# A gated scan and a two-layer product on one core: v released by the first piece of alpha, a new written order for all engines at the start, and idle products ahead of four steps

## The chip, the cores and the metric

The kernel runs on one core of a Trainium2 chip. The metric is the device time of one execution in microseconds; before the change it is 177.0, the median of 5 runs (176.86 to 177.19). A core has five engines with queues of their own: TensorE (PE in the profile, its weight loads PEld), VectorE (DVE), ScalarE (ACT), GpSimd (POOL) and SyncE (SP). Each works through its own instructions in program order and waits for the others through semaphores. SP, ACT and POOL also issue DMA transfers.

## The reference, cut to what matters

A scan over 768 steps for 4 batches and 8 heads of width 48, then two products with a GELU between them:

```python
for t in range(S):
    state = alpha[:, :, t, :, None] * state + np.einsum('bhd,bhe->bhde', k[:, :, t], v[:, :, t])
    y[:, :, t] = np.einsum('bhd,bhde->bhe', q[:, :, t], state)
x = np.ascontiguousarray(y.transpose(0, 2, 1, 3)).reshape(B * S, H * D)      # 3072 x 384
h = x @ w_in                                                                  # 384 -> 2048
g = 0.5 * h * (1.0 + np.tanh(c * (h + 0.044715 * h * h * h)))
return (g @ w_out).astype(np.float32)                                         # 2048 -> 384
```

Inputs and output are float32.

## The kernel before, in words

**Tiling.** The 768 steps are cut into 6 chunks of 128. A "pair" is one chunk of two batches, so there are 12 pairs, numbered in the order of the chunks: pairs 0 and 1 are chunk 0. In a chunk the scan is done with matrix products. ScalarE takes the logarithm of alpha (`ln`, L359/L361), TensorE sums it along the steps with a triangular matrix (`cum`, L346 to L380), ScalarE takes the exponentials b, binv and bend of the sums (L401, L407), VectorE scales q by b and k by binv (`qp`, `kp`, L418). TensorE turns both (`t`, L428), a copy brings them to SBUF (`ev`, L446), TensorE forms the products of all step pairs (`attn`, L489), VectorE masks them to the lower triangle (`mask`, L496). TensorE makes y from the masked products and v, and from chunk 1 on also from the carried state (`y`, L543, L546); kv (L506) and st (L528, L531) carry the state on. y is cast (`x`, L553), turned (`tx`, L560) and copied (`xe`, L564) to xT. In pairs 0 and 1, which are loaded in a packed form, k is also turned back (L454, L461), and v comes in float32 and is cast by a copy (`vb`, L389).

**The two layers.** `l1` is layer 1 (L572, tile hT): groups of six products of 256 columns, each followed by a GELU on ScalarE (L578). Eight groups make a pair. w_in comes in four pieces; group n of a pair needs piece n // 2, and all x of its pair. `l2` is layer 2 (L591, tile acc): four products of 384 columns a group; w_out comes in four pieces as well. `ot` copies a result out (L603) and SP stores it. Chunk 0's two pairs share their layer 2.

**PSUM.** Three kinds of banks: `ca` (one double bank, sums and products), `yk` (two: turns, y, kv, x turns) and `ff` (four: hT, acc, and the sums and products of the first pairs). A task that takes a bank waits for the one that used it before.

**Loads.** The alpha, q and k of pairs 0 and 1 come in twelve loads of 192 KB, ten from SP's queue and two (the first q and k) from ScalarE's: the "ring". They are named `load.0` to `load.11`. Everything else goes through POOL's queue in the order of `LOADS`: v of pair 0 (`load.12`), the first piece of w_in, v of pair 1, the other three pieces, w_out and the rows of later pairs. Two `gate` tasks stand in this queue. A gate is a copy of one column (L314) on POOL out of a tile that a ring load fills: it waits for that load, so all that POOL issues behind it waits too. `gatea 0 1` reads the second half of pair 0's alpha, and stands ahead of v; `gatek 0 1` reads the second half of pair 0's k, and stands ahead of w_in. From the ninth transfer on POOL waits for the landing of the one eight earlier before it issues.

**Order.** All work is added as tasks to a `Scheduler`, which fixes every engine's program. The list `FIRST` is taken first, word for word: `P:` is TensorE, `V:` VectorE, `A:` ScalarE, `G:` POOL, `S:` SP, and `fill.n` are n idle products of 512 columns of zeros in an ff bank (L289). Behind the list the scheduler goes on by itself, task by task, by priority and by planned times; for these it uses `COST`, `LAT`, and for the loads the planned landings in `LANDED`. A task that can run on ScalarE or VectorE goes where the list puts it.

Of the kernel before, what the change touches and what calls it, by code (L numbers as in the profile page):

```python
# [171 lines left out]
class _Kernel:  # L172
# [3 lines left out]

    SPLIT = (2,)
    EARLY = (0, 1)
    LOADS = ('gatea 0 1', 'v0', 'gatek 0 1', 'in 0', 'v1', 'in 1', 'in 2', 'in 3', 'out 0', 'out 1', '2a', 'out 2', '2b', 'out 3', '3', '4', '5', '6', '7', '8', '9', '10', '11')

    PACKED, CUM_FF, R = (0, 1), (0, 1), 4
    RINGS = (('a', 0, 0, 1), ('a', 0, 1, 2), ('q', 0, 0, 1), ('k', 0, 0, 1), ('q', 0, 1, 2), ('k', 0, 1, 2),
             ('a', 1, 0, 1), ('a', 1, 1, 2), ('q', 1, 0, 1), ('k', 1, 0, 1), ('q', 1, 1, 2), ('k', 1, 1, 2))
    BY_ACT = (2, 3,)

    FIRST = """
        A:table.0 A:load.2 A:load.3 S:load.0 S:load.1 S:load.4 A:ln0.0 S:load.5 P:fill.7 P:cum0.0 A:ln0.1 G:gate.0 G:load.12 S:load.6 P:cum0.1 A:b0.0 S:load.7
        A:bend0.0 V:qp0.0 A:binv0.0 A:binv0.1 S:load.8 V:kp0.0 P:fill.2 P:t0.0 A:b0.1 V:ev0.0 P:fill.1 P:t0.1 S:load.9 A:ev0.1 V:qp0.1 S:load.10 A:bend0.1
        P:fill.3 P:attn0.0 V:kp0.1 G:gate.1 S:load.11 P:t0.2 G:load.13 V:mask0.0 A:ev0.2 P:t0.3 G:load.14 V:mask0.1 A:ev0.3 P:fill.1 P:t0.4 V:ev0.4 P:fill.1
        P:attn0.1 A:ln1.0 G:load.15 P:t0.5 V:mask0.3 P:cum1.0 A:ev0.5 G:load.16 V:vb0.0 A:ln1.1 V:end0.0 P:y0.0 V:mask0.2 G:load.17 P:kv0.0 A:binv1.0 P:cum1.1  # L190
        V:st0.0 A:x0.0 G:load.18 A:vb0.1 V:kp1.0 P:tx0.0 A:b1.0 P:y0.1 V:xe0.0 G:load.19 V:qp1.0 P:t1.1 A:x0.1 A:bend1.0 G:load.20 A:b1.1 P:fill.1 P:t1.0
        A:ev1.0 V:ev1.1 G:load.21 V:qp1.1 P:fill.1 P:kv0.1 V:st0.1 G:load.22 A:binv1.1 P:tx0.1 P:attn1.0 V:xe0.1 G:load.23 P:t1.2 V:kp1.1 P:l10.0 A:ev1.2
        G:load.24 V:mask1.0 P:t1.3 A:bend1.1 P:t1.4 V:mask1.1 G:load.25 A:ev1.3 P:l10.1 V:ev1.4 G:load.26 A:vb1.0 P:t1.5 P:attn1.1 G:load.27 V:ev1.5 P:y1.0
        G:load.28 P:l10.3 V:end1.0 V:vb1.1 V:mask1.2 G:load.29 A:gelu0.0 P:kv1.0 P:l10.2 V:mask1.3 A:x1.0 G:load.30 P:l10.5 A:gelu0.1 V:st1.0 A:gelu0.3 P:y1.1
        G:load.31 P:l10.4 A:gelu0.5 V:x1.1 P:tx1.0 A:gelu0.2 P:tx1.1 P:l10.6 G:load.32 V:xe1.1 A:gelu0.4 V:xe1.0 P:l10.7 A:gelu0.6 G:load.33 P:l11.0 A:gelu0.7
        P:l11.6 A:gelu1.0 P:l11.5 A:gelu1.6 P:l11.7 A:gelu1.5 P:l11.2 A:gelu1.7 P:l11.4 A:gelu1.2 P:l11.3 A:gelu1.4 P:l11.1 A:gelu1.3 P:kv1.1 P:l20.0
        A:gelu1.1 P:l20.4 P:l20.1 A:ln2.0 P:l20.2 P:cum2.0 P:l20.5 A:b2.0 A:binv2.0 P:l20.9 A:bend2.0 V:kp2.0 A:ln2.1 P:l20.6 V:st1.1 P:cum2.1 V:qp2.0 P:l20.8
        A:b2.1 A:binv2.1 P:t2.0 P:l20.3 V:kp2.1 A:ev2.0 V:qp2.1 P:l20.10 A:bend2.1 P:attn2.0 P:t2.1 V:mask2.1 P:l20.7 A:ev2.1 V:mask2.0 P:l20.14 A:ln3.0
        P:attn2.1 P:y2.0 V:mask2.2 P:l20.13 V:mask2.3 P:l20.12 V:x2.0 P:cum3.0 A:ot0.0 V:ot0.1 P:y2.1 A:ot0.2 S:store0.0 S:store0.1 P:tx2.0 P:l20.11 A:x2.1
        S:store0.2 V:xe2.0 A:b3.0 P:tx2.1 P:l20.15 V:xe2.1 A:binv3.0 V:end2.0 P:l12.0 V:ot0.3 A:bend3.0 P:l12.1 V:qp3.0 S:store0.3 P:kv2.0 P:l12.2 V:st2.0  # L200
        A:gelu2.0 P:l12.3 V:end3.0 V:kp3.0 A:gelu2.1 P:l12.4 A:gelu2.2 P:t3.0 A:gelu2.3 P:t3.1 A:gelu2.4 V:ev3.0 P:l12.5
    """.split()
    LANDED = {"load.0": 2800, "load.1": 3400, "load.2": 4400, "load.3": 5000, "load.4": 6000, "load.5": 7300, "load.12": 10100, "load.6": 9200, "load.7":
              10000, "load.8": 10500, "load.9": 11000, "load.10": 11600, "load.11": 12000, "load.13": 14100, "load.14": 16000, "load.15":
              17800, "load.16": 19200, "load.17": 21100, "load.18": 23500, "load.19": 24800, "load.20": 26400, "load.21": 27100, "load.22":
              27900, "load.23": 28300, "load.24": 30100, "load.25": 31000, "load.26": 31900, "load.27": 32600, "load.28": 32900, "load.29":
              34800, "load.30": 36700, "load.31": 38400, "load.32": 41200, "load.33": 42600}

    NARROW = (0, 1)

# [12 lines left out]
                a=6, q=5, k=5, vb=6)  # L223
# [60 lines left out]
    def fill(self, n):  # L284
# [4 lines left out]
                self.nc.tensor.matmul(ps, self.zero[:, 0:self.C], self.zero, start=True, stop=True)  # L289
        return emit  # L290


    def load(self, n, c, i, lo=0, hi=2):

# [202 lines left out]
                                         self.ut[:, None, :].to_broadcast([self.C, self.H // 2, self.C]), op=ALU.mult)  # L497
        return emit

    def kv(self, u, i):  # L500
        nc, H, C, D = self.nc, self.H, self.C, self.D

        def emit(e):
            kv = u["kv", i] = self.tile("yk", [C, H // 2, 2 * D], F32, "kv")
            for p in range(H // 2):
                nc.tensor.matmul(kv[:, p, :], u["kn" if u["packed"] else "kp"][:, i, 2 * p:2 * p + 2, :].rearrange("t h d -> t (h d)"),  # L506
                                 u["vb"][:, i, 2 * p:2 * p + 2, :].rearrange("t h d -> t (h d)"),
                                 start=True, stop=True)
        return emit
# [25 lines left out]
    def y(self, u, i, c, b):  # L535
        nc, H, C, D = self.nc, self.H, self.C, self.D

        def emit(e):
            y = u["y", i] = self.tile("yk", [C, H, D], F32, "yps")
            if c > 0:  # L540
                st = self.state[b][c % 2]
                for p in range(H // 2):
                    nc.tensor.matmul(y[:, 2 * p:2 * p + 2, :], u["T"][:, 0, i, p, :], st[:, p, :],  # L543
                                     start=p == 0, stop=False, skip_group_check=True)
            for h in range(H):
                nc.tensor.matmul(y[:, h, :], u["atm", i][:, h % 2, h // 2, :], u["vb"][:, i, h, :],  # L546
                                 start=c == 0, stop=True, skip_group_check=True)
        return emit
# [4 lines left out]
            self.copy(e)(x, u["y", i].rearrange("t h d -> t (h d)"))  # L553
        return emit

    def turn_x(self, u, i):
        def emit(e):
            ps = u["xT_ps", i] = self.tile("yk", [self.C, self.NKT, self.C], BF16, "xT_ps")
            for j in range(self.NKT):
                self.nc.tensor.transpose(ps[:, j, :], u["x", i][:, j * self.C:(j + 1) * self.C], self.ident)  # L560
        return emit
# [57 lines left out]
    def tasks(self):  # L619
        s = self.s = Scheduler(self.BUFS, self.fill, 60000, self.FIRST, self.LANDED)  # L620
# [6 lines left out]
        loads, n, gate, held = {}, 0, [], {}  # L627
# [43 lines left out]
        for m, (c, i) in enumerate(pairs):  # L671
# [81 lines left out]
            for j in range(2):  # L753
                b, o, k, ms, turned = 2 * i + j, P + 10 + 3 * j, kp[j], masks[j], turns[j]
                at = ats[m][-1 if m not in self.SINGLE else j]
                y = s.add("y", {"PE": W["intra"] + (W["inter"] if c else 0)}, P + 20 + j, self.y(u, j, c, b),
                          ms + turned + [vin[j]] + ([states[b, c - 1]] if c else []))
                xc = s.add("x", {"ACT": W["xc_act"], "DVE": W["xc"]}, P + 20 + j, self.x(u, j), [y])
                if m in self.TURN_X:
                    xe = tx = s.add("turn", {"SP": W["turn"]}, P + 22 + j, self.turn_x_dma(u, j, c, b), [xc], xbar=W["xbar_x"], late=W["late_x"] * (m < 6))  # L760
                else:
                    tx = s.add("tx", {"PE": W["tx"]}, P + 22 + j, self.turn_x(u, j), [xc])
                    xe = s.add("xe", {"DVE": W["xe"]}, P + 22 + j, self.turned_x(u, j, c, b), [tx])
                    tx.take("yk", xe)
                y.take("yk", xc)
                xc.take("x", tx)
                users += [at, y]
                ms[0].take("atm", y)
                xts[c, b], ys[b, c] = xe, y
                vs.append(y)  # L770
                if c < NCH - 1:
                    if u["packed"]:
                        tb = s.add("t", {"PE": W["t4"]}, P + 29 + j, self.turn_back(u, j), turned)
                        k = s.add("ev", {"DVE": W["ev4"], "ACT": W["ev4_act"]}, P + 29 + j, self.turned_back(u, j), [tb])
                        tb.take("yk", k)
                        users.append(tb)
                        backs.append(tb)
                    kv = s.add("kv", {"PE": W["kv"]}, P + 30 + j, self.kv(u, j), [k, vin[j]])
                    st = states[b, c] = s.add("st", {"DVE": W["st" if c else "st0"]}, P + 30 + j, self.carry(u, j, c, b),
                                              [kv, end] + ([states[b, c - 1], ys[b, c - 1]] if c else []))  # L780
                    kv.take("yk", st)
                    vs.append(kv)
                    kvs.append(kv)
                    cs.append(st)
# [136 lines left out]
```

## Time and profile before

| | |
|---|---|
| time, median of 5 runs | 177.0 us (176.86 to 177.19) |
| the profiled execution | 177.78 us |
| its span on the core | 176.0 us |
| TensorE busy | 170.9 us (97%) |
| ScalarE, VectorE, POOL busy | 128.8, 96.4, 57.6 us |
| TensorE's share of the chain that ended last | 86% |
| DMA's share of it | 9% |
| granted TensorE clock | 1.00 |

The span runs from the first to the last instruction; 1.78 us of the profiled time lie around it. Most of TensorE's time is layer 1 (69.7 us in 576 products) and layer 2 (69.0 us in 416). "Busy" of TensorE is modelled from pipelined products, so a product counts longer than the distance to the next one, and small gaps don't show in it; the chain of work that ended last gives the distances. In a row of the timeline the first number is the start, the second the length, and what stands in brackets is the idle time of the engine just before, with what ended it. For a DMA that ScalarE, SP or POOL issues, the row is the issue; the transfer lands later.

### The profile page before, as it was taken

What the parts mean: (1) busy time and instruction counts of PE and PEld (TensorE: products, weight loads), DVE (VectorE), ACT (ScalarE), POOL (GpSimd) and SP (SyncE); (2) the same over time, 40 slices, a digit from 0 to 9 for tenths busy, and PEclk for the clock granted to TensorE, in tenths of its full rate; (3) what the DMA queues carried; (4) which work ended last, traced back from release to release, by engine and by line L of the source; (5) the groups of instructions that cost most, each with busy time, mean ns of one, the idle gap of its engine ahead of it and who ended that gap; (6) DMA issues with size and microseconds to landing.
All of it is one profiled execution on the core that took longest, in us unless ns stands there. A gap on an engine that the chain in (4) does not pass through costs nothing.

```text
span 176.0 us, 4440 instructions
## 1 busy us (share of the span) xinstructions
PE 170.9 (97%) x1845; PEld 135.1 (77%) x1845; DVE 96.4 (55%) x192; ACT 128.8 (73%) x213; POOL 57.6 (33%) x64
## 2 busy tenths in 40 slices
PE   7999899999999999999999999999999999999993
PEld 2576799666886897797698698688697697796973
DVE  6599720265878994696598797494436405000000
ACT  4677979766968668858788967977988984481841
POOL 2495447987645766667530000000000000000000
PEclk9999999999999999999999999999999999999999
DMA  4999999999999999999999993371271360301102
GB/s 141 312 246 219 210 242 238 236 211 206 230 291 206 236 262 217 216 224 204 196 257 231 200 114 98 63 171 49 47 180 34 89 164 4 108 27 48 45 0 89
DMA packets 49620, 28.86 MB, mean 164 GB/s; under 512 B 37696, under 2 KB 46016, under 8 KB 49600
## 3 DMA queue, kind: packets, MB, share of 16 engines
q0 software_dynamic: 26464, 17.70, 60.8%
q1 hardware_dynamic: 22592, 10.49, 24.8%
q10 hardware_dynamic: 544, 0.39, 0.8%
q8 instruction: 14, 0.23, 0.6%
q14 instruction: 6, 0.05, 0.1%
HBM read 25.17 MB, written 4.72 MB: 170 GB/s over the span
## 4 chain that ended last, share of the span: by engine, by line
PE 86%; DMA 9%; POOL 2%; SPq 1%; issue 0%; ACT 0%; POOLq 0%
PE acc L591 36%; PE hT L572 35%; DMA w_in<-in_moe_w_in_dram 6%; PE at L489 3%; DMA k<-in_k_dram 3%; PE qkT_ps L428 3%; PE yps L546 2%; PE yps L543 2%; PE cum L378 2%; PE kv L506 2%; SPq L305 1%; PE xT_ps L560 1%; POOL w_in L321 1%; PE cum L380 1%; POOL v L308 1%
## 5 line engine op out<-in xcount | busy, mean ns | idle before, releaser
L572 PE MATMUL hT<-xT,w_in 128*128 128x256 bf16 x576 | 69.7, 273 | 0.5 <-DMA w_in<-in_moe_w_in_dram 0.5
L578 ACT ACTIVATE gT<-hT 128x512 bf16<-128x512 f32 x96 | 56.4, 598 | 18.5 <-PE hT L572 15.1
L591 PE MATMUL acc<-w_out,gT 128*128 128x384 bf16 (+3 forms) x416 | 69.0, 313 | 0.0
L572 PEld LDWEIGHTS <-w_in 128*128 128x128 bf16 x576 | 61.0, 114 | 2.5 <-DMA w_in<-in_moe_w_in_dram 0.8
L591 PEld LDWEIGHTS <-gT 128*128 128x128 bf16 x416 | 36.9, 97 | 19.2
L496 DVE TENSOR_TENSOR atm<-at,ut 128x512 bf16<-128x512 f32 x48 | 30.1, 683 | 12.7 <-PE at L489 12.6
L418 DVE TENSOR_TENSOR qp<-q,b 128x768 bf16<-128x768 f32 (+1 forms) x15 | 11.9, 794 | 13.8 <-ACT b L407 13.8
L418 DVE TENSOR_TENSOR kp<-k,binv 128x768 bf16<-128x768 f32 (+1 forms) x15 | 11.9, 792 | 11.0 <-ACT binv L407 10.6
L603 ACT COPY ot<-acc 128x384 f32<-128x384 f32 (+3 forms) x17 | 7.4, 439 | 13.0 <-PE acc L591 12.9
L308 POOL DMA_DIRECT2D k<-in_k_dram x11 | 12.2, 1105 | 7.0 <-DMA vb<-in_v_dram 2.4
L308 POOL DMA_DIRECT2D vb<-in_v_dram x11 | 12.1, 1101 | 7.1 <-DMA a<-in_alpha_dram 2.4
L308 POOL DMA_DIRECT2D q<-in_q_dram x11 | 12.2, 1107 | 6.7 <-DMA w_in<-in_moe_w_in_dram 1.4
L308 POOL DMA_DIRECT2D a<-in_alpha_dram x11 | 12.2, 1113 | 5.2 <-DMA w_in<-in_moe_w_in_dram 1.4
L407 ACT ACTIVATE b<-cum 128x768 bf16<-128x768 f32 (+1 forms) x15 | 10.3, 685 | 3.3 <-PE cum L380 2.3
L280 ACT ACT_TABLE_LOAD x9 | 11.5, 1283 | 0.9 <-PEq L905 0.7
L578 ACT ACT_TABLE_LOAD x9 | 11.5, 1283 | 0.2
L407 ACT ACTIVATE binv<-cum 128x768 bf16<-128x768 f32 (+1 forms) x15 | 10.1, 682 | 0.0
L528 DVE TENSOR_TENSOR stmp<-kv,st 128x384 f32<-128x384 f32 x16 | 8.9, 553 | 2.0 <-PE kv L506 2.0
L553 DVE CAST x<-yps 128x384 bf16<-128x384 f32 x12 | 6.7, 557 | 5.8 <-PE yps L546 5.7
L446 ACT COPY qkT<-qkT_ps 128x512 bf16<-128x512 bf16 (+1 forms) x9 | 6.5, 728 | 4.1 <-PE qkT_ps L428 4.0
L531 DVE TENSOR_TENSOR st<-stmp,ends 128x384 bf16<-128x384 f32 x16 | 8.9, 558 | 0.6
L546 PE MATMUL yps<-vb,atm 128*128 128x48 bf16 x192 | 8.7, 183 | 0.1
(65 smaller groups left out, 155.8 us busy)
## 6 DMA issues: line engine op xcount, KB each, us to landing
out_dram<-ot SPq DMA_DIRECT2D x19, 192.0 KB, 5.3
a<-in_alpha_dram POOLq DMA_DIRECT2D x9, 384.0 KB, 11.8
q<-in_q_dram POOLq DMA_DIRECT2D x9, 384.0 KB, 11.9
k<-in_k_dram POOLq DMA_DIRECT2D x9, 384.0 KB, 11.9
vb<-in_v_dram POOLq DMA_DIRECT2D x9, 192.0 KB, 11.9
w_in<-in_moe_w_in_dram POOLq DMA_DIRECT2D x4, 384.0 KB, 9.9
w_out<-in_moe_w_out_dram POOLq DMA_DIRECT2D x4, 384.0 KB, 11.3
out_dram<-ot SPq DMA_DIRECT2D x9, 96.0 KB, 1.8
```

What stands on the lines that cost most here:

```text
L280: nc.scalar.add_instruction(mybir.InstLoadActFuncSet(name=nc.get_next_instruction_name(), act_func_set_id=i, engine=mybir.EngineType.Activ ...
L308: dma(u[t][:, lo:hi].rearrange("t b h d -> t (b h) d"), src.rearrange("b h s d -> s (b h) d")[c * C:(c + 1) * C])
L407: self.nc.scalar.activation(u[n].rearrange("t i h d -> t i (h d)")[:, lo:hi], cum, AF.Exp, scale=1.0 if n == "b" else -1.0)
L418: self.nc.vector.tensor_tensor(out, rows, b, op=ALU.mult)
L496: self.nc.vector.tensor_tensor(u["atm", i][:, o], u["at", i][o], self.ut[:, None, :].to_broadcast([self.C, self.H // 2, self.C]), op=ALU.mult)
L528: nc.vector.tensor_tensor(s, acc, old, op=ALU.add)
L531: nc.vector.tensor_tensor(new.rearrange("f p (o d) -> f (p o) d", o=2), acc.rearrange("f p (o d) -> f (p o) d", o=2), ends, op=ALU.mult)
L546: nc.tensor.matmul(y[:, h, :], u["atm", i][:, h % 2, h // 2, :], u["vb"][:, i, h, :], start=c == 0, stop=True, skip_group_check=True)
L572: self.nc.tensor.matmul(h[:, s], w_in[:, j, nt % 4 + s], self.xT[c % self.NX][:, j, lo:hi].rearrange("p g t -> p (g t)"), start=j == 0, st ...
L578: return lambda e: self.nc.scalar.activation(self.gT[c % self.NG][:, nt:nt + 2, lo * self.C:hi * self.C], f.pop(("h", c, lo, nt)), AF.Gelu ...
L591: self.nc.tensor.matmul(f["acc", c, b][:, lo:hi], self.gT[c % self.NG][:, nt, b * self.C:(b + 1) * self.C], self.w_out[:, nt, lo:hi], star ...
L603: self.copy(e)(f["ot", c, b][:, sl], f["acc", c, b] if half is None else f["acc", c, b, half][:, sl])
```

## The change

1. In `LOADS`, `gatea 0 1` becomes `gatea 0 0`: the gate in front of v of pair 0 reads the first half of pair 0's alpha instead of the second.
2. `FIRST` is replaced by another order, and `LANDED` by other planned landings. On ScalarE the two ring loads are now issued ahead of the table load. On VectorE both scalings of q and k of pair 0 come ahead of the first copy of a turn. On TensorE the sums of pair 1 move up, and two turns move. In pair 1 the x turn of the first batch moves ahead of the groups of the third w_in piece, the last turn of k behind the first of these groups, and one group of pair 0 (`l10.6`) behind all of pair 1's. In layer 2 of chunk 0 another sequence of groups stands between the tasks of pairs 2 and 3. Three casts of v, four of the copies `ev` of pairs 0 and 1 and both of pair 2, and some casts of x and copies of results change between ScalarE and VectorE.
3. Seventeen idle products in ff banks become fourteen. New are idle products in the bank of the step that follows them (`warm`): six turns of the identity ahead of the first x turn, and one product of 384 columns of zeros each ahead of y of batches 0 and 1, and of kv of batch 0. Their values are overwritten.

What is computed, the bytes moved, and POOL's and SP's issue order stay as they were.

```diff
-    LOADS = ('gatea 0 1', 'v0', 'gatek 0 1', 'in 0', 'v1', 'in 1', ...
+    LOADS = ('gatea 0 0', 'v0', 'gatek 0 1', 'in 0', 'v1', 'in 1', ...
+    WARM = {("tx", 0): 6, ("y", 0): 1, ("kv", 0): 1, ("y", 1): 1}
     FIRST = """
-        A:table.0 A:load.2 A:load.3 S:load.0 S:load.1 S:load.4 A:ln0.0 S:load.5 P:fill.7 P:cum0.0 A:ln0.1 G:gate.0 G:load.12 ...
...
-        A:ev1.0 V:ev1.1 G:load.21 V:qp1.1 P:fill.1 P:kv0.1 V:st0.1 G:load.22 A:binv1.1 P:tx0.1 P:attn1.0 V:xe0.1 G:load.23 P:t1.2 V:kp1.1 P:l10.0 A:ev1.2
-        G:load.24 V:mask1.0 P:t1.3 A:bend1.1 P:t1.4 V:mask1.1 G:load.25 A:ev1.3 P:l10.1 V:ev1.4 G:load.26 A:vb1.0 P:t1.5 P:attn1.1 G:load.27 V:ev1.5 P:y1.0
-        G:load.28 P:l10.3 V:end1.0 V:vb1.1 V:mask1.2 G:load.29 A:gelu0.0 P:kv1.0 P:l10.2 V:mask1.3 A:x1.0 G:load.30 P:l10.5 A:gelu0.1 V:st1.0 A:gelu0.3 P:y1.1
-        G:load.31 P:l10.4 A:gelu0.5 V:x1.1 P:tx1.0 A:gelu0.2 P:tx1.1 P:l10.6 G:load.32 V:xe1.1 A:gelu0.4 V:xe1.0 P:l10.7 A:gelu0.6 G:load.33 P:l11.0 A:gelu0.7
...
+        A:load.2 S:load.0 A:load.3 S:load.1 A:table.0 S:load.4 S:load.5 S:load.6 A:ln0.0 G:gate.0 G:load.12 S:load.7 P:fill.7 P:cum0.0 A:ln0.1 S:load.8
...
+        P:fill.1 P:t1.1 A:x0.1 V:qp1.1 A:ev1.1 G:load.22 P:fill.1 P:kv0.1 V:st0.1 G:load.23 A:bend1.1 P:fill.1 P:tx0.1 P:attn1.0 V:xe0.1 G:load.24 P:t1.2 V:mask1.0
+        P:t1.3 A:ev1.2 P:l10.0 G:load.25 V:mask1.1 A:ev1.3 P:t1.4 G:load.26 P:l10.1 V:vb1.0 V:ev1.4 G:load.27 P:y1.0 P:attn1.1 V:end1.0 G:load.28 V:x1.0
+        P:kv1.0 G:load.29 A:gelu0.0 V:mask1.2 P:l10.3 A:vb1.1 V:st1.0 P:tx1.0 G:load.30 P:l10.2 A:gelu0.3 V:mask1.3 A:gelu0.1 P:l10.5 V:xe1.0 G:load.31
+        A:gelu0.2 P:y1.1 P:t1.5 A:gelu0.5 V:x1.1 P:l10.4 G:load.32 P:tx1.1 P:l10.7 A:gelu0.4 V:xe1.1 V:ev1.5 G:load.33 P:l11.0 A:gelu0.7 P:l11.7 A:gelu1.0
...
+    def warm(self, key, bank, c, b):
+        width = bank.shape[1] * bank.shape[2]
+        for _ in range(self.WARM.get((key, b), 0) if c == 0 else 0):
+            self.nc.tensor.matmul(bank, self.zero[:, 0:self.C],
+                                  self.zero[:, 0:width].rearrange("p (a b) -> p a b", a=bank.shape[1]), start=True, stop=True)
...
             kv = u["kv", i] = self.tile("yk", [C, H // 2, 2 * D], F32, "kv")
+            self.warm("kv", kv, c, b)
...
             y = u["y", i] = self.tile("yk", [C, H, D], F32, "yps")
+            self.warm("y", y, c, b)
...
             ps = u["xT_ps", i] = self.tile("yk", [self.C, self.NKT, self.C], BF16, "xT_ps")
+            for _ in range(self.WARM.get(("tx", b), 0) if c == 0 else 0):
+                self.nc.tensor.transpose(ps[:, 0, :], self.ident, self.ident)
```

Group names in the list: `l10.n` is group n of layer 1 of pair 0, `l11.n` of pair 1, `l20.n` are the groups of layer 2 of chunk 0.

## The prediction, made before the changed kernel was run

> **What bounds the kernel now.** I read three views in this order: the chain that ended last, the timeline of the first 24 us, and the busy time with the DMA share by stretches of 1 us. First the chain (start, length, what):
>
> ```profile
> 2.86 4.92 DMA k<-in_k_dram
> ...
> 7.92 0.18 POOL gate L314
> ...
> 8.39 0.74 POOL w_in L321
> 9.13 1.17 POOL v L308
> ...
> 11.03 10.48 DMA w_in<-in_moe_w_in_dram
> ...
> 21.56 0.85 PE hT L572 x6
> 22.41 0.20 PE yps L546 x8
> 22.61 0.67 PE hT L572 x6
> 23.27 0.34 PE xT_ps L560 x6
> 23.61 6.64 PE hT L572 x60
> ```
>
> Up to 21.5 us the chain is a row of transfers: k of pair 0 lands at 2.86 + 4.92 = 7.78, the gate on POOL lets the weights go, and the third piece of w_in lands at 11.03 + 10.48 = 21.51. From 21.56 on it is TensorE alone up to 173.4, without a gap worth naming. So the end is the moment at which the weights let TensorE start its unbroken run, plus the work left then. The timeline shows the other three waits:
>
> ```profile
> 11.83 0.35 DVE L389 CAST vb<-v 128x384 bf16<-128x384 f32 x1
> ...
> 16.65 0.82 PE L572 MATMUL hT<-xT,w_in 128*128 128x256 bf16 x6
> ...
> 19.67 0.30 PE L572 MATMUL hT<-xT,w_in 128*128 128x256 bf16 x1 [0.24 <-DMA w_in<-in_moe_w_in_dram]
> ...
> 23.74 0.90 POOL L308 DMA_DIRECT2D a<-in_alpha_dram  x1 [1.39 <-DMA w_in<-in_moe_w_in_dram]
> ```
>
> TensorE waits at 19.67 for the second piece of w_in; POOL's wait before 23.74 is for the fourth, which its landing time (11.80 + 11.7, the longest of the four) puts at 23.5. The cast of v at 11.83 has no idle time before it, although v landed at 5.23 + 6.2 = 11.4: VectorE, not v, set that time. Last, the DMA engines (last but one column their share, 1.00 is full, then GB/s) and what the two queues moved from 8 to 10 us:
>
> ```profile
> 5.00:6.00 1.00, 1.00 (x14) 0.85 (x13) 0.00 (x0) 0.76 (x2) 0.89 (x2) 1.00 0.90 270
> 6.00:7.00 1.00, 1.00 (x14) 0.59 (x13) 0.56 (x1) 1.00 (x5) 0.51 (x1) 1.00 1.07 356
> 7.00:8.00 1.00, 0.74 (x10) 0.41 (x9) 0.84 (x2) 0.46 (x2) 0.08 (x1) 1.00 0.97 323
> 9.00:10.00 1.00, 1.00 (x17) 0.63 (x14) 0.96 (x3) 0.39 (x1) 1.00 (x2) 1.00 1.06 300
> ```
> ```profile
> q0 software_dynamic: 94, 0.35, 57.3%
> q1 hardware_dynamic: 405, 0.29, 50.0%
> ```
>
> The engines are full from 3 us on, before v's first packet moves.
>
> **Part 1, v released by the first alpha.** Before, the gate copies at 5.11, just after the second piece of alpha lands at 5.06, and v is issued at 5.23. The first piece lets ScalarE's Ln start at 3.76, so the gate goes to about 3.8 and v to 3.9, 1.3 us sooner. No packet of POOL's queue moves between 6 and 8 us in the trace, so its first packet comes 2.8 us after the issue: at 6.7 instead of 8.0. There is no idle transfer time at 6.7 to fill (shares 1.07 and 0.97), so v takes the place of ring loads (the 192 KB loads of SP and ScalarE). The bytes in front of each w_in piece stay the same: twelve ring loads and v are 2.75 MB either way. If the engines stay full, w_in lands when it did: change 0. On SP's queue one wait moves: the eleventh ring load (q of pair 1, its second half) was issued at 7.30, held by a semaphore that q of pair 0 had from its second half, landed at 7.29; the changed program deals the semaphores out anew, and it waits for the first half, landed at 4.34. So SP may issue it 1.1 us sooner, right behind the tenth (5.51 + 0.61). That keeps the ring's queue filled and reorders nothing inside it: 0.
>
> The gate in front of w_in waits for k of pair 0 (7.78), and it stays. That load now shares with v, and everything on POOL behind that gate (w_in, the second v, w_out, the next rows) slips with it. Here a rule and the rows differ. The Trainium skill, DMA: Bandwidth & Descriptors, section Queues, rings and completion order, says that each DMA engine takes turns between its queues, a whole packet at a time. By that rule alone each of v's 3.7 KB packets (0.35 MB by 94) goes in front of one ring packet of 0.72 KB, and k would wait for all of v: 393 KB at the 350 GB/s of the stretch 6 to 7 is 1.1 us. The rows say less: v's bytes come over 2 us (0.35 MB from 8 to 10), so in the 1.1 us between 6.7 and k's landing about half of v passes, 0.55 us. I take 0.5, ends 0.2 and 1.1.
>
> Does that slip cost w_in anything? W_in's first piece is issued at 8.39 and, with the same 2.8 us, can move from 11.2; after, from 11.7. By when are ring and v through? The stretches from 2 to 9 us (119, 361, 289, 270, 356, 323 and 345 GB/s) moved 2.06 of the 2.75 MB; the other 0.69 takes 2.3 us at the 300 GB/s of 9 to 10, so until 11.3 when nothing else is queued. That leaves the engines a hole of 0.4 us by the middle value, 0.1 at the low end and 1.0 at the high end. Against it, from 9 to 12 they gave 300, 259 and 239 GB/s while the queues mixed; with less mixing, 0.7 MB at 300 instead of at the mean of 266 wins 0.3 back. Value for w_in's landings: 0.4 - 0.3, **+0.1 us**; ends -0.3 (won, no hole) and +1.0 (full hole, nothing won).
>
> **Part 2, the new order on all engines.** What counts is the work TensorE has between the first hT group and the fourth piece of w_in. Before, from 16.65 to 23.5 (6.85 us), in the chain's own lengths: six hT groups of six products at 0.11 (6.64 by 60), 3.96; three turns of 4 products at 0.22, 0.66; attention 0.33; two y 0.40; kv 0.17; two x turns 0.34: 5.86. So TensorE idles 1.0 us there, waiting for weights. After, the same six groups with two turns 0.44, attention 0.33, two y, kv and two x turns: 5.64. So this stretch may begin 6.85 - 5.64 = 1.2 us later without moving the end. The set left behind the fourth piece is the same: two hT groups of pair 0, eight of pair 1, one kv, all of layer 2. So the order moves nothing by itself, as long as pair 0 is not over 1.2 us late. It isn't: k's second half is used by VectorE at 8.70, 0.9 after its landing, which covers a slip of 0.5. ScalarE now loads its table behind its two issues (they wait for a memset at 1.15, and end at 2.55), so the table ends at 2.6 + 1.28 = 3.9 and Ln starts 0.1 late: inside the 1.2.
>
> Between the third piece (21.51) and the fourth (23.5) the new order has hT, y, one turn, hT and one x turn: 0.66 + 0.20 + 0.22 + 0.66 + 0.17 = 1.9, with two x turns in place of the turn before: fits. Behind the fourth piece only one hT group (0.66) instead of two stands ahead of the first group of pair 1, which needs the last turned x: turn at 23.2, copy 0.35 on VectorE from 23.65, so 24.1; the group ends at 23.5 + 0.66 = 24.2. No gap, with 0.1 to spare; I charge **0.05 us**. From 24 to 60 us eight copies and casts change between ScalarE and VectorE. TensorE is full there (8.00 of 8.00), and the hT and acc groups cover them; if the cover fails at one place, it is one copy's difference, 1.01 on ScalarE against 0.69 on VectorE for a turned pair: ends -0.1 and +0.3, value 0. From 68 us on TensorE keeps its order.
>
> **Part 3, idle products.** Seventeen products of 512 columns become fourteen, and nine new ones stand ahead of y, kv and the x turn of pair 0: six of 128 columns at 0.055 (4 turns in 0.22) and three of 384 at 0.164 (256 columns take 0.11): 0.83 added, 0.65 removed (0.216 each). All lie before 15 us, where TensorE waits for ScalarE and VectorE. If pair 0 is late they add up to 0.8 to it, still behind the 1.2: 0.
>
> **Sum.** Against the profiled execution (176.0 span, 1.78 around it, 177.78): +0.1 + 0.05 + 0 = 177.9. The runs' median is 0.78 below that execution, so 177.0 + 0.15, rounded to **177.1 us**. If the weights land that much sooner in the runs than under the profiler, the 1.0 us of waiting shrinks to 0.2 and pair 0's lateness shows sooner: that is why the range leans upward.
>
> **Rivals.**
> - *Weights sooner.* Less mixing wins 0.3 to 0.8 for w_in, and the 1.0 us of idle lets TensorE use up to all of it: 176.5. For: 239 GB/s at 11 to 12 is poor against 356. Against: full engines and unchanged bytes.
> - *The gate slips by all of v* (the rule's case). k lands at 8.9, w_in is issued 1.1 later, and nothing moves for 1.0 us after the ring is through: 177.0 + 1.0 - 0.3 = 177.7. It decides from a slip of about 0.5 on; below that the ring still fills the engines. For: v's packets are five times as long. Against: v trickles in.
> - *The clock falls back.* The seven first products take 3.17, 0.45 each, against 0.216 later, though the granted clock reads 1.00 throughout. The skill's TensorE: Matmul & The Clock Gate, Part 1, says that the array starts at half clock, and returns to it after an idle window of about 3.4 us. If fewer idle products let that happen once, the 2.5 us of work from 12 to 16 double, less 1.2 of slack: +1.3, 178.3. The rows show idle stretches under 1 us at a time, so without the return the sum has 0 here.
> - *Nothing moves*: landings within 0.1, 177.0.
>
> **Chances.** My forecast and "nothing moves", both inside 0.2% (0.35 us, about what a measurement of this kernel can tell from no change), 0.43; weights sooner 0.25; gate slip 0.24; clock 0.03; a stall of the new order after 24 us 0.05. So faster 0.25, same 0.43, slower 0.32. Range for 8 in 10: from 176.3 (0.7 us of the gain) to 177.9 (the full slip with one lost cover); within the likeliest case alone 176.7 to 177.4.
>
> **What would show it.** In the trace after: v issued near 3.9; k of pair 0 landing at 8.0 to 8.9 and the second gate with it; the third and fourth w_in within 0.3 us of 21.5 and 23.5; hT waits for w_in still there, ahead of the unbroken run. I am wrong if TensorE no longer waits for w_in at all (then pair 0 or pair 1 decides), if w_in moves by more than 0.5, or if gaps of over 0.1 us stand on TensorE behind 24 us.

## The result, and the profile after

The changed kernel takes 177.92 us (median of 42 runs, 177.24 to 181.74) against 177.16 (77 runs, 176.34 to 178.71) of the kernel before in the same session. The ratio is 1.0036, with a 95% interval of 1.0026 to 1.0046: **0.64 us slower** (0.46 to 0.81). The ratio and its interval are an estimate over the session and not the quotient of the two medians, which would be 1.0043, or 0.76 us; the differences below go by the ratio. The run of 181.74, at a granted clock of 0.981, is a slow one, and the ratio leaves it out, as it does one of experiment 8. The profiled execution takes 178.49, with a span of 176.7 and a granted clock of 1.00, against 177.78 and 176.0.

One landmark in the trace splits this difference: the start of the 96th product of layer 1, the last one of pairs 0 and 1. It is at 29.98 before and at 30.17 after, +0.19. From there to the start of the last product of layer 2 ("the late part" below) it is 143.15 before and 143.68 after, **+0.53**. Together 0.72, the 0.7 by which the spans differ.

First the late part. The chain that ended last after the change (start, length, what), in the stretch that the forecast had taken as covered (three dots stand for lines left out):

```profile
45.08 0.66 PE hT L585 x6
45.73 0.18 PE kv L516 x4
45.92 0.02 issue
45.94 0.57 DVE stmp L538
46.51 0.02 issue
46.53 0.56 DVE st L541
47.09 0.87 DVE qp L427
47.96 0.48 DVE stmp L538
...
48.94 0.96 DVE kp L427
49.90 0.05 issue
49.95 0.84 PE qkT_ps L437 x12
50.79 0.65 PE hT L585 x6
```

and the same place before:

```profile
46.20 1.96 PE hT L572 x18
48.16 0.22 PE qkT_ps L428 x4
48.38 0.01 issue
48.40 0.84 PE qkT_ps L428 x12
49.24 0.65 PE hT L572 x6
```

The chain leaves TensorE and goes over VectorE: two carries (stmp and st), with q of pair 3 scaled between them, and only then k of pair 3 (kp), for which TensorE's turn waits. The timeline of TensorE after shows the hole:

```profile
49.02 0.39 PE L437 MATMUL qkT_ps<-ident,qp 128*128 128x128 bf16 x4
49.95 0.40 PE L437 MATMUL qkT_ps<-ident,kp 128*128 128x128 bf16 x4 [0.54 <-DVE kp L427]
```

Second the early part. Here the chain is this (the same columns), and below it stand four rows of the timeline:

```profile
16.45 0.55 DVE qp L427
17.00 0.48 DVE st L541
17.52 0.65 PE qkT_ps L437 x8
18.17 0.66 PE hT L585 x6
...
21.33 1.31 PE hT L585 x12
22.64 0.20 PE yps L557 x8
22.84 0.23 PE k_ps L463 x4
23.07 0.66 PE hT L585 x6
23.72 0.17 PE xT_ps L573 x3
23.89 6.55 PE hT L585 x60
```
```profile
3.90 1.28 POOL L317 DMA_DIRECT2D v<-in_v_dram  x1
15.97 0.56 DVE L427 TENSOR_TENSOR kp<-k,binv 128x384 bf16<-128x384 f32 x1 [1.10 <-ACT qkT L455]
18.01 0.82 PE L585 MATMUL hT<-xT,w_in 128*128 128x256 bf16 x6
22.65 0.90 POOL L317 DMA_DIRECT2D a<-in_alpha_dram  x1 [1.32 <-DMA w_in<-in_moe_w_in_dram]
```

v is issued at 3.90. The third and fourth pieces of w_in land at 20.49 and 22.37, about 1.0 sooner than the 21.51 and 23.46 of before; POOL's issue behind the fourth moves with it, from 23.74 to 22.65. No transfer stands in the chain any more: from the first hT at 18.01 TensorE runs through, and pair 0's own steps set that start. In this execution the second half of pair 1's k landed as late as 15.88 (12.45 before), and the row at 15.97 waited for it, with the carry and the x copy of pair 0 behind it on VectorE. The bracket names a copy of ScalarE, which ended at about the same time; in the second trace of this kernel the same row starts at 15.10, ahead of that copy (15.66), so it doesn't wait for the copy.

### The profile page after: what moved, and what is told of

The parts are those of the page before. It is cut to its first block, busy times and chain, and to the rows that moved or that the text cites. A ratio compares the mean times of both kernels' runs of the same rounds, so it can differ in the third digit from the quotient of the medians.

```text
span 176.7 us, 4453 instructions
## 1 busy us (share of the span) xinstructions
PE 170.5 (96%) x1851; PEld 135.7 (77%) x1851; DVE 96.4 (55%) x192; ACT 128.3 (73%) x213; POOL 57.6 (33%) x64
## 4 chain that ended last, share of the span: by engine, by line
PE 91%; DVE 3%; ACT 3%; issue 1%; ACTq 1%
PE acc L604 36%; PE hT L585 34%; PE at L498 4%; PE qkT_ps L437 3%; PE yps L557 3%; PE kv L516 2%; PE yps L554 2%; PE cum L387 2%; PE cum L355 2%; PE xT_ps L573 1%; DVE qp L427 1%; ACT L282 1%; PE cum L389 1%; ACTq L314 1%; DVE st L541 1%
## 5 line engine op out<-in xcount | busy, mean ns | idle before, releaser
L616 ACT COPY ot<-acc 128x384 f32<-128x384 f32 (+3 forms) x18 | 8.0, 442 | 14.5 <-PE acc L604 14.3
L370 ACT ACTIVATE la<-a 128x768 f16<-128x768 f32 (+1 forms) x11 | 8.5, 785 | 0.6 <-DMA a<-in_alpha_dram 0.6
```

Source lines behind the costliest of these rows:

```text
L370: self.nc.scalar.activation(u["la"][:, lo:hi, :, 0:self.D], u["a"][:, lo:hi], AF.Ln)
```

## The experiments

After these two traces my theory had two terms: some 0.2 us in the early part, where the late k holds pair 0, and some 0.5 in the late part, where kp of pair 3 stands behind two carries. The rivals put the loss on the gate, on the idle products, or on the new order of pairs 0 and 1 as a whole. "Late part" is defined above. Differences in microseconds are ratios to the kernel before times 177.16.

**1. The same two kernels once more, one profile each.** No edit.

> The kernel before, unchanged, for a second profile. In the six profiles so far the fourth piece of w_in lands at 23.5 (before), 22.4 (changed), 22.3 (changed with the late gate), 22.2, 22.6 and 22.6: not in step with the gate. My theory: the landing differs from execution to execution, whatever the gate, and 23.5 was a late one; then it lands below 23.2 here, and TensorE's run starts sooner by the same amount. Rival, the kernel before has late weights by its order: 23.3 to 23.6 again.

> The changed kernel, unchanged, for a second profile. The last ring load (second half of k of pair 1) landed at 15.9 in its first profile, but at 12.3 to 13.0 in four kernels with the same or nearly the same issues. Theory: 15.9 belonged to that execution; here it lands near 12.5, the first hT group starts near 17.2, and the wait of 0.5 us ahead of the turn of k of pair 3 (near 49) is there again. Rival: 15.9 and 18.0 again, so term one is real in this kernel.

Measured: before again 177.56, late part 143.15, fourth piece of w_in at 23.22, between what the theory named (below 23.2) and what the rival did (23.3 to 23.6). After again 177.84, late part 143.68; the second half of pair 1's k landed at 12.57, the first hT came at 17.34, w_in's fourth piece at 22.61. So the late k was one execution's, while the +0.53 of the late part came back to a hundredth. Without the late k the early part is even 0.23 shorter after the change than before: its end is at 29.50 in this second trace and at 29.73 in the second one of before. The chain of this second trace holds no transfer either:

```profile
15.66 0.59 ACT qkT L455
16.29 0.33 PE xT_ps L573 x3
16.62 0.33 PE at L498 x8
16.95 0.55 PE qkT_ps L437 x8
17.50 0.66 PE hT L585 x6
```

**2. The late part: VectorE's order behind the first carry.**

```diff
-  V:st2.0 A:gelu2.0 P:l12.2 V:qp3.0 A:gelu2.1 P:l12.3 V:st2.1 A:gelu2.2 P:l12.4 V:kp3.0
+  V:st2.1 A:gelu2.0 P:l12.2 V:qp3.0 A:gelu2.1 P:l12.3 V:kp3.0 A:gelu2.2 P:l12.4 V:st2.0
```

> The changed kernel, but on VectorE the carry of batch 3 (its bank is needed first) and then both scalings of pair 3 come ahead of the carry of batch 2. TensorE's program is the same. If term two is that stall: TensorE's wait of 0.54 us ahead of the turn of k near 49.9 goes, 0.4 to 0.5 us faster than the changed kernel, 0.2 to 0.3 slower than before. Rival, the stall is taken up by a later wait: within 0.1 of the changed kernel, 0.6 to 0.8 slower than before.

Measured: 177.29 us, ratio 1.0004 (0.9984 to 1.0023), late part 142.96. TensorE's program is the same; in the chain its sixteen turns now stand in one piece:

```profile
45.06 3.27 PE hT L585 x30
48.34 0.89 PE qkT_ps L437 x16
49.23 0.65 PE hT L585 x6
```

From the first turn to the next hT it is 0.89 here, 1.08 before (49.24 - 48.16), and 1.61 after (50.79 less 49.18, where the thirty products begun at 45.91 end). The differences, 0.19 and 0.72, are those of the late parts: 143.15 and 143.68 against 142.96. So the stall of the new order is this one place, and the order of before loses 0.19 in the same place.

**3. Which of the two moves does it.** Only kp3.0 and st2.1 change places; st2.0 stays first.

```diff
-  V:st2.0 ... P:l12.3 V:st2.1 A:gelu2.2 P:l12.4 V:kp3.0
+  V:st2.0 ... P:l12.3 V:kp3.0 A:gelu2.2 P:l12.4 V:st2.1
```

> The changed kernel with one move: on VectorE the scaled k of unit 3 (kp3.0) stands ahead of the carry st2.1, and st2.0 stays the first of the two carries. Time from the last hT group of layer 1 to the last acc group (143.68 in the changed kernel, 143.15 in the one before, 142.96 with both moves). Theory, that TensorE waits behind VectorE's queue alone (kp3.0 is what its turn needs, and the carry stood 1.1 us ahead of it): 142.9 to 143.2. Rival, that TensorE's turn also needs the bank which kv2.1 took first and which st2.1 sets free: 143.5 to 143.8, because st2.1 now ends later than kp3.0 did. One execution; only the late part counts.

Measured: late part 142.96, time 176.87 (one run). The rival, that the bank taken by kv2.1 holds the turn, falls. VectorE's timeline:

```profile
46.07 0.95 DVE L427 TENSOR_TENSOR qp<-q,b 128x768 bf16<-128x768 f32 x1
46.94 0.95 DVE L427 TENSOR_TENSOR kp<-k,binv 128x768 bf16<-128x768 f32 x1
47.81 0.55 DVE L538 TENSOR_TENSOR stmp<-kv,st 128x384 f32<-128x384 f32 x1
48.39 0.56 DVE L541 TENSOR_TENSOR st<-stmp,ends 128x384 bf16<-128x384 f32 x1
48.87 0.68 DVE L455 COPY qkT<-qkT_ps 128x1024 bf16<-128x1024 bf16 x1
```

One carry is two instructions, about 1.1 us, and it is enough that it stands behind kp instead of ahead of it.

**4. The old start with the new middle.** The order of before up to the last kv of pair 1, from there the new one with both moves of experiment 2; the gate as before, no idle products ahead of y, kv and x turn.

```diff
-  ... P:kv1.1 P:l20.0 A:gelu1.1 P:l20.4 P:l20.1 A:ln2.0 P:l20.2 (the rest of before)
+  ... P:kv1.1 P:l20.0 A:gelu1.1 V:st1.1 P:l20.1 P:l20.3 A:ln2.0 P:l20.2 P:cum2.0 (the rest of after, with st swapped)
```

> The kernel before up to the last kv of pair 1 (old gate, old order, no new idle products), and from layer 2 of chunk 0 on the order of the change with the two carries of the state swapped as in the run that took the stall away. In that run's profile the stretch from the end of layer 1 of pair 1 to the end took 0.2 us less than in the kernel before (143.8 against 144.0 by my count of the last product less the 96th of layer 1). If the new middle is better by itself: 0.1 to 0.3 faster than before. Rival, the gain was of that execution: same as before within 0.1.

Measured: 176.89 us, ratio 0.9994 (0.9972 to 1.0016), late part 142.96. The late part gained what it should; the interval is too wide to tell its 0.19 from nothing.

**5. The new start with the old middle.** The reverse: the changed kernel up to the last kv of pair 1, then the order of before.

```diff
-  ... P:kv1.1 P:l20.3 A:gelu0.6 V:st1.1 P:l20.0 P:l20.2 (the rest of after)
+  ... P:kv1.1 P:l20.0 A:gelu0.6 P:l20.4 P:l20.1 A:ln2.0 P:l20.2 (the rest of before)
```

> The changed kernel's order, early gate and idle products up to the last kv of pair 1, and the order of before from there on. Theory, that the loss is the late stall alone and the new start gains and loses about nothing: late part 143.15, time 0.0 to +0.2 us against before, ratio 1.000 to 1.001. Rival, that the new order of pair 0 and pair 1 costs part of it too: ratio 1.002 or more. Second rival, that the sooner weights are a gain which the late stall hides: 0.998 or less.

Measured: 177.65 us, ratio 1.0027 (1.0016 to 1.0037), late part 143.15. The first theory, that the start is free, missed: the rival's 1.002 is reached. So the new start costs something too, +0.48 (0.28 to 0.66) in these runs, while in its trace w_in's fourth piece lands at 23.56, 0.1 later than in the first trace of before.

**6. The gate alone, both ways.** In the changed kernel the gate is put back to the second alpha; in the kernel before it is moved to the first.

```diff
-    LOADS = ('gatea 0 0', 'v0', ...      (changed kernel)
+    LOADS = ('gatea 0 1', 'v0', ...
```
```diff
-    LOADS = ('gatea 0 1', 'v0', ...      (kernel before)
+    LOADS = ('gatea 0 0', 'v0', ...
```

> The changed kernel with the first gate back on the second half of alpha; order and idle products of the change stay. My theory after the two traces: the loss of 0.7 us has two terms. Term one, 0.2 us: v and w_in move sooner, so the last ring load (k of pair 1, second half) lands at 15.9 instead of 12.4; VectorE waits for it ahead of the copy of x of pair 0, and the first hT group starts at 18.0 instead of 16.6. Term two, 0.5 us: behind 45 us the scaling of k of pair 3 stands behind two carries of the state on VectorE, and TensorE waits for it. If so: k lands near 12.5 again, first hT near 16.7, third piece of w_in back near 21.5, only term two stays: 0.5 us slower than the kernel before (0.3 to 0.6). Rival, the early gate makes the whole loss: same as before within 0.1.

> The kernel before with the gate of v on the first half of alpha and nothing else changed. My theory: v and the weights land about 1.0 us sooner (third piece of w_in near 20.5), the last ring load late; but in this order the copy of x stands ahead of the scaling that needs this load, so nothing is held, and the unbroken run starts up to 0.9 us sooner: 0.5 to 0.9 us faster than before. Rival, the early gate itself costs through the late ring loads: 0.2 to 0.7 us slower. Second rival, the 1.0 us of w_in comes from the other order and not from the gate: same within 0.1.

Measured: 177.83 us, ratio 1.0018 (1.0007 to 1.0030), which is +0.32, at the low end of the 0.3 to 0.6 that were expected (the medians alone differ by 0.53); the rival, no loss with the late gate, lies just outside the interval. But its trace is not the one that was expected: the third piece of w_in lands at 20.35 and not near 21.5, and the first hT comes at 17.56 and not near 16.7, so the late gate alone doesn't bring the old landings back. And 177.19 us, ratio 0.9995 (0.9979 to 1.0012), where a gain of 0.5 to 0.9 was expected: a plain miss. The trace of the second looks like the gain, w_in's fourth piece at 22.20 and layer 1 of the first two pairs ended at 28.77, and its profiled execution took 176.57, 0.6 less than the median of its own 22 runs. The expectation had read one execution as if it were the kernel.

**7. The old start with the early gate and the new middle.** As 4, with the gate at the first alpha.

> The order of before up to the last kv of pair 1, with v's gate at the first alpha, then the new order with both moves on VectorE (kp3.0 and st2.1 ahead of st2.0). No idle products ahead of y, kv and x turn. Late part 142.96 by every theory, 0.19 below before. Theory, that the sooner weights (0.7 to 1.2 us in the traces) help an order whose pair 0 is ready at 16.4 to 16.7: another 0.3 to 0.6 below, ratio 0.9955 to 0.9975. Rival, that outside the profile the early gate is worth nothing (as in the run with it alone, 0.9995): ratio 0.9985 to 0.9995.

Measured: 177.17 us, ratio 1.0000 (0.9987 to 1.0012), late part 142.96. The rival is nearer than the theory: again the early gate shows no gain.

**8. The x copy of pair 0's second batch put ahead of pair 1's k on VectorE.**

```diff
-  P:y0.1 A:b1.1 V:kp1.1 G:load.21 ... V:xe0.1 G:load.24 P:t1.2 V:mask1.0 P:t1.3 A:ev1.2 P:l10.0
+  P:y0.1 A:b1.1 G:load.21 ... V:xe0.1 V:kp1.1 G:load.24 P:t1.2 V:mask1.0 P:l10.0 A:ev1.2 P:t1.3
```

> The changed kernel, but VectorE takes the second half of k of pair 1 behind the copy of x of pair 0 instead of ahead of it, and TensorE takes the first hT group ahead of the turn of that k. If the wait for this k holds pair 0 (term one), the first hT group starts near 16.8 and the earlier weights can be used: 0.7 to 1.0 us faster than the changed kernel, 0.1 to 0.3 faster than before. Rival, weights or the chain of pair 1 set the start of the unbroken run: within 0.2 of the changed kernel, 0.5 to 0.7 slower than before.

Measured: 178.02 us, ratio 1.0034 (1.0022 to 1.0046), late part 143.68: no gain. Guarding pair 0 against the late k is worth nothing in the runs; in the trace this k landed at 12.51, in time.

**9. The idle products ahead of y, kv and x turn taken out,** from the changed kernel alone and together with the moves of experiment 2.

```diff
-    WARM = {("tx", 0): 6, ("y", 0): 1, ("kv", 0): 1, ("y", 1): 1}
+    WARM = {}
```

> The changed kernel without the nine new idle products ahead of y, kv and the x turn; the order stays. If they lie in time that TensorE has to spare: within 0.15 us of the changed kernel, 0.5 to 0.8 slower than before. Rival, they stand on pair 0's chain (the product ahead of kv goes only when the bank is free, and puts 0.16 in front of kv, and so of the turns behind it): 0.2 to 0.4 faster than the changed kernel. Second rival, they hold the clock up: without them slower by 0.3 or more.

> The changed kernel with both moves on VectorE and without the nine idle products ahead of y, kv and x turn of pair 0. Late part 142.96. Theory, that the idle products stand in pair 0's own chain and make its first hT late (16.64 without them against 17.1 to 17.5 with them): 0.2 to 0.5 below the changed kernel with the moves alone, ratio to before 0.9975 to 0.9995. Rival, that they cost nothing because TensorE waits anyway: ratio as with the moves alone, 1.0000 to 1.0010.

Measured: 177.73 us, ratio 1.0033 (1.0012 to 1.0053), late part 143.68; and 177.16 us, ratio 1.0002 (0.9989 to 1.0014), late part 142.96. Against 1.0036 and 1.0004 with the idle products, nothing that the runs can tell. In the traces they do cost: from the first sum of pair 1 (cum L355) to the first hT it is 7.51 us in five traces with them (the first of after, with its late k, and experiment 8, with another order, are left aside) and 7.23 or 7.24 in the two without, so 0.28 of their 0.83 lies in pair 0's own chain. It is a cost of one start, hidden or not by what the weights do.

**The early part of all traces in one table.** One execution each, microseconds from the span's start. "k" is the landing of the second half of pair 0's k; "w_in" that of its fourth piece; "first hT" and "end" are the starts of the first and of the 96th product of layer 1.

| start, gate | kernel | k | first hT | hT less k | w_in | w_in + 6.51 | first hT + C | end |
|---|---|---|---|---|---|---|---|---|
| old, late | before | 7.79 | 16.65 | 8.86 | 23.46 | **29.97** | 29.06 | 29.98 |
| | before again | 7.94 | 16.76 | 8.82 | 23.22 | **29.73** | 29.17 | 29.73 |
| | experiment 4 | 7.73 | 16.57 | 8.84 | 22.92 | **29.43** | 28.98 | 29.43 |
| old, early | 6, second | 7.47 | 16.36 | 8.89 | 22.20 | 28.71 | **28.77** | 28.77 |
| | 7 | 8.15 | 17.11 | 8.96 | 22.43 | 28.94 | **29.52** | 29.51 |
| new, late | 6, first | 7.58 | 17.56 | 9.98 | 22.27 | 28.78 | **29.72** | 29.72 |
| new, early | after | 7.47 | 18.01 | 10.54 | 22.37 | 28.88 | **30.17** | 30.17 |
| | after again | 8.00 | 17.34 | 9.34 | 22.61 | 29.12 | **29.50** | 29.50 |
| | 2 | 7.80 | 17.17 | 9.37 | 22.58 | 29.09 | **29.33** | 29.33 |
| | 3 | 7.66 | 17.07 | 9.41 | 22.26 | 28.77 | **29.23** | 29.23 |
| | 5 | 8.28 | 17.63 | 9.35 | 23.56 | **30.07** | 29.79 | 30.10 |
| new, no idle | 9, first | 7.57 | 16.64 | 9.07 | 22.43 | **28.94** | 28.80 | 28.99 |
| | 9, second | 8.27 | 17.34 | 9.07 | 22.15 | 28.66 | **29.50** | 29.50 |

C is 12.41 for the old start and 12.16 for the new, read off the rows where pair 0 decides. The end is the later of the two columns, to 0.05, in every row: either the weights hold TensorE, or pair 0's first hT does. The fourth piece stands here as a measure; the wait itself is for the third (21.51 before, and the product behind it at 21.56), which lands 1.86 to 1.95 sooner in every trace. (Experiment 8 has other steps between and a C of its own, 12.52.) The old start with the late gate was held by the weights, nearly all others by pair 0. And the new start brings the first hT 9.34 to 9.41 behind k in four of its six rows, the old one 8.82 to 8.96: **0.5 later**, of which about 0.3 are the idle products; for the other 0.2 no single step is shown. The two other rows are after, with the late k of pair 1, and the first of 6, whose chain begins at the second half of alpha, landed at 5.43 (4.77 to 5.24 in the other rows of this start), and whose seven sums behind it take 1.24 us, against 0.82 in experiment 2. Where pair 0 decides, only 0.25 of the 0.5 reaches the end, because C is 0.25 shorter.

The landing of k is a yardstick here and not shown to be what sets pair 0's start. Followed back from the first hT, the chain begins at the second half of alpha in experiments 2, 3 and 7 (landed at 5.17, 5.24 and 6.03), at the first half of k in the second of 9 (7.54), and at no transfer in both traces of after.

Experiment 5 is the row where the weights did hold the new order, shown again as a chain:

```profile
2.86 5.42 DMA k<-in_k_dram
...
11.53 10.16 DMA w_in<-in_moe_w_in_dram
21.68 0.04 issue
21.73 0.85 PE hT L585 x6
...
23.82 6.55 PE hT L585 x60
```

**What follows from all of them.** The late stall is shown: the late part is 143.68 in all five traces with the new middle, 142.96 in all five with kp moved ahead, and 143.15 in all four with the old middle, each to a hundredth. The two pairs of timed kernels that differ in it alone (after and experiment 2, and the two of 9) differ by 0.57 and 0.55, where the traces say 0.72; intervals of about 0.4 to each side leave out zero and cover that. Against the kernel before, the stall is by the traces 0.53 of the 0.64.

The early part is not settled. Taken as the timed difference less the late part of the traces, it is +0.11 for after, +0.07 for 8, +0.05 for the first of 9, +0.48 for 5, -0.21 for the first of 6, +0.26 for 2 and +0.23 for the second of 9: on the mean +0.14, with intervals of 0.2 to 0.4 to each side of each. With the old start it is -0.09 to +0.19. So no gain of the new start is shown, and a loss stands clear of zero in experiment 5 alone (0.28 to 0.66). The table gives 0.25 later for the new start when pair 0 decides in both orders, at the same landings; against the kernel before this doesn't hold, for there the weights decided, with ends of 29.43 to 29.98 in three traces, and the five traces of the new start with the early gate and its idle products end at 29.23 to 30.17, with nearly the same mean (29.71 and 29.67). What the early part costs in the timed runs stays open: a profile shows the landings of one execution, and none shows those of the timed runs.

## Why the prediction was right or wrong

The time, 177.92, came at the upper end of the range (177.9), and on the side that the forecast gave 0.32, not in its likeliest case. The forecast started from 177.0 for the kernel before, which took 177.16 in the same session; as a difference it said about +0.1, and +0.64 came. That the range holds the time is luck in good part. Its upper end was made for the full slip of the gate with one lost cover on top: the slip didn't come, and the cover that was lost cost more than its upper end. Step by step:

- **v's issue near 3.9:** right, 3.90. SP's eleventh ring load went out sooner, 6.38 instead of 7.30, as said.
- **k of pair 0 slips by 0.5 (0.2 to 1.1):** too much. It landed at 7.47 and 8.00 in the two traces of after, and over the ten traces with the early gate at 7.47 to 8.28, mean 7.87, against 7.58 to 7.94, mean 7.76, over the four with the late one. So the slip is about 0.1, inside the scatter. The rule of the Trainium skill (DMA: Bandwidth & Descriptors, Queues, rings and completion order), taken alone, would have put k at 8.9; no trace shows that (the latest is 8.28), and the smaller slip that the forecast took from the rows was still too large. The rival *the gate slips by all of v* is out.
- **w_in lands when it did (+0.1, -0.3 to +1.0):** outside its ends in both traces of after, where the fourth piece came at 22.37 and 22.61, against 23.46 and 23.22. But the gate isn't shown to be the cause. With the old start the three traces of the late gate (22.92 to 23.46) do stand above the two of the early one (22.20 and 22.43); with the new start the late gate has 22.27 and experiment 5 with the early one 23.56. The forecast took one landing time as the kernel's own; over the ten traces with the early gate it spreads by 1.4.
- **Pair 0 isn't over 1.2 late, so its lateness costs nothing:** the working was good and its input was not. The work ahead of the fourth piece was given as 5.86 before and 5.64 after; the table gives 12.41 - 6.51 = 5.90 and 12.16 - 6.51 = 5.65. But the slack of 1.2 hung on w_in at 23.5. With w_in near 22.4 it is about 0.1 (22.4 less 16.65 less 5.65), and the 0.5 by which the first hT is later uses up most of what the sooner weights would have won. Of that 0.5, 0.3 are the idle products, which Part 3 priced at 0 by the same slack. The forecast named this case ("pair 0's lateness shows sooner"), leant its range upward for it and gave it no price.
- **0.05 us at the first group of pair 1:** right in size. Where the weights held the new order the end came 6.54 and 6.56 behind the fourth piece, against 6.51 in the old.
- **"From 24 to 60 us eight copies/casts change", value 0, ends -0.1 and +0.3:** this is the step that failed. TensorE was full there before, and the forecast took the engines that serve it as covered by that. The reason the cover failed was not one of the copies but the place of a task between two others: a second carry, 1.1 us, stood ahead of kp of pair 3. It measured +0.53, above its upper end. In the cases it stood as *a stall of the new order after 24 us*, at 0.05.
- **Nothing moves** and **weights sooner** fall, the second because, by the table, pair 0 took over where the weights came sooner. **The clock falls back** falls too, by the lengths of the products: behind 7 us all are as short as in the kernel before, with the idle products and without, such as the eight products of y in 0.36 or 0.37 in all 14 traces. The granted clock can't decide this, for it reads 1.00 as well over the first sums, which take longer:

```profile
4.45 1.44 PE L355 MATMUL cum<-la,ut_blk 128*128 128x384 f16 x7
12.06 0.36 PE L557 MATMUL yps<-vb,atm 128*128 128x48 bf16 x8
```

- Of the three signs named for being wrong, both traces of after show all: no wait for w_in at all, w_in moved by over 0.5, a gap over 0.1 behind 24 us (0.54 and 0.55).

So "no change" was wrong by one term of the sum, the late stall, and right for the start only within what its traces scatter.

## What to carry to other kernels

When an order is replaced on all engines, "the bottleneck engine is full there" is no cover: walk the queue of every engine that feeds it, and add up what now stands ahead of each result that it waits for; here one carry of two instructions ahead of a scaling cost 0.53 us. When a slack rests on a DMA's landing, take that landing from several executions before spending the slack, and price the case in which it is gone. And a profile split at one landmark behind the last wait for a transfer separates what repeats to a hundredth from what doesn't.

## What the runs showed of the hardware

The landing of a transfer moves far more between executions than the work behind the last wait for one. The second half of pair 1's k landed at 15.88 in one execution of the changed kernel and at 12.57 in the other. w_in's fourth piece landed between 22.26 and 23.56 in five traces with the same start and the same gate (both of after, experiments 2, 3 and 5), and between 22.15 and 23.56 over all 14 traces, which issue it at 11.48 to 12.29. In all 14 the 143 us behind the last wait for a transfer repeated within 0.01 for each order.

TensorE's first products also differ between executions. The first seven sums (cum L355) take 1.44 us in both traces of after and 0.82 in experiments 3 and 5, which have the same tasks up to there; the next seven take 1.24 in the first of 6, 1.11 in the second trace of after and 0.82 in experiments 2, 3 and 5. The profile's granted clock reads 1.00 for the fast and for the slow ones (4.4 to 5.9 us, after and experiment 3).
